# Loading ak, b and rv as whole 128-row tiles instead of two 40-row halves, without the start memsets (delta-rule attention followed by a GELU MLP, one core)

## The chip, the cores and the metric

The kernel runs on one core of a Trainium2 chip, in one launch. The metric is the device time of one execution in microseconds. The three runs of the kernel before took 675.35, 676.0 and 679.76 us, a median of 676.0 us. All tensors are 32-bit floats.

## The reference, cut to what matters

The first block is a recurrent attention over 768 time steps, for 4 batches of 8 heads with a head size of 40. The second is a two-layer MLP over the 3072 tokens that the first gives.

```python
state = np.zeros((B, H, D, D))                  # B, H, S, D = 4, 8, 768, 40
for t in range(S):
    y[:, :, t] = np.einsum('bhd,bhde->bhe', rt, state)
    Sa = np.einsum('bhde,bhe->bhd', state, at)
    state_decay = state * wt[:, :, None, :] - np.einsum('bhd,bhe->bhde', Sa, bt)
    state = state_decay + np.einsum('bhd,bhe->bhde', vt, kt)
x = y.transpose(0, 2, 1, 3).reshape(B * S, H * D)   # 3072 x 320
h = x @ w_in                                        # 320 -> 2048
g = h * (1.0 / (1.0 + np.exp(-1.702 * h)))
return g @ w_out                                    # 2048 -> 320
```

## The kernel before, in words

The sequence is cut into 12 chunks of 64 steps. A chunk is worked on for two batches at a time, so there are 24 units (chunk, batch pair). Inside a unit the recurrence is turned into matrix work: cumulated decays (`decay`), scores between the steps of the chunk (`prep`, tiles ps_A, ps_RV, and ps_N in `inverse`), the inverse of a triangular 64x64 matrix per head by repeated squaring (`inverse`, tile ps_level, with transposes EX on VectorE in between), and the update of the state and the outputs (`solve`, tiles ps_B, ps_X, ps_y). After each second unit a chunk of tokens is complete, and its MLP (`mlp`, tiles ps_up and ps_down) becomes available as matmul work between the units.

TensorE (PE) works on tiles of 64x64 or less, four of them beside each other, so a tile has two halves of 64 partitions. For the tensors that are laid out by channel, each half holds one head's 40 channels in its first 40 rows, and 24 rows that are zero.

Four things matter for the change:

- **The loads (L495 to L505).** For each unit i, `load(i)` plans five transfers, all issued on SP's queue: ak (a and k side by side, 128x1024 elements in SBUF), b (128x512), rv (r and v, 128x1024), RV (v by time, 128x320) and time (128x640). RV and time are loaded as 128 rows in one transfer. Of ak, b and rv only the rows 0 to 39 and 64 to 103 are loaded, in two transfers of 40 rows each (L498 to L503, `HALF` is rows 0 to 63 and 64 to 127). In HBM these three tensors have 128 rows per unit, with zeros in the 48 others. A row is 4096 bytes for ak and rv, and 2048 bytes for b. Each of the three has two buffers in SBUF, used in turn by even and odd units.
- **The memsets (L334, L335, L339, L340, L348, L349).** VectorE (DVE) sets both buffers of ak and both of b to zero at the start, since the element operations of `prep` (L619, L621, L624) run over all 128 rows. The buffers of rv are not set: only their 40-row parts are read, by matmuls.
- **The order.** `ORDER` (L107 on) lists all planned tasks by number, in one order that was written out ahead; each engine executes its own tasks in that order. SP's queue carries all loads, the weights (`weight`, L469: raw 64-bit pieces of 128x320 elements of the MLP's weights, 32 transfers, all of them among the first loads), the stores of the MLP's input to HBM and its loads back (L971, L975), and the stores of the result (L1019). The program gives the transfers eight completion semaphores in turn: before a transfer is issued, SP waits until the transfer eight places ahead of it has landed, besides waiting until its buffer is free.
- **The weights.** The MLP's weights come as 64-bit floats and are turned into 32-bit ones on ACT (L447), DVE (L451, L455, L459) and POOL (L463) in the first part of the run.

Unit 0's path at the start goes: logw is loaded and its logarithm taken (L526), PE cumulates it (ps_cumc), ACT makes the decay factors FT and GT (L565), DVE multiplies ak by GT and FT (L624, L619) and b by GT (L621), and PE computes ps_RV, ps_A and ps_N. Every matmul is issued by the helper `mm`, so PE's rows all bear L300.

Of the kernel before, what the change touches and what calls it, by code (L numbers as in the profile page):

```python
# [248 lines left out]
def rwkv7_gelu_quick(ctx: ExitStack, tc: tile.TileContext, time_d, v_d, w_d, wc_d, ak_d, b_d, rv_d, w_in, w_out, out):  # L249
    nc = tc.nc  # L250
    H, D, S = 8, 40, out.shape[0] // 4
# [17 lines left out]
    HALF = [slice(0, 64), slice(64, 128)]  # L269
# [10 lines left out]
    plan = Plan(dict(logw=3, wc=3, G=1, wch=3, wz=2, time=2, ak=2, b=2, rv=2, FT=3, GT=1, kh=2, bh=2, zr=2, rz=2,  # L280
                     A=1, B=1, RV=2, E0=2, W0=2, P21=2, PT=2, W=2, E=2, ES=2, EX=2, T=2, Tc=1, QT=1, zraw=2, zT=1, M=2, x=1, xT=3, g=4, ob=1), 4)
# [44 lines left out]
    def of(e):  # L326
        return nc.gpsimd if e == "POOL" else nc.vector


    def several(name, shape):  # L330
        return [single(f"{name}{i}", shape) for i in range(plan.slots[name])]

    ak_t, b_t, rv_t = several("ak", [128, 2, 8, 64]), several("b", [128, 8, 64]), several("rv", [128, 2, 8, 64])
    def padded(engine, t):  # L334
        engine.memset(t, 0.0)  # L335

    nc.scalar.preload_act_table_set("natural_log_exp_and_others")

    padded(nc.vector, ak_t[0])  # L339
    padded(nc.vector, b_t[0])  # L340
    full = work.tile([128, 128], FP32, tag="g0", name="full")
    make_identity(nc, full)
    ident = single("ident", [128, 64])
# [1 line left out]
    one32, two32 = single("one32", [128, 32]), single("two32", [128, 32])  # L345
    nc.vector.tensor_add(one32, ident[:, :32], ident[:, 32:])
    nc.vector.tensor_add(two32, one32, one32)
    padded(nc.vector, ak_t[1])  # L348
    padded(nc.vector, b_t[1])  # L349

    def select(t, compare, base, sign, fill):

# [142 lines left out]
    def load(i):  # L495
        for name, of, src, n in (("ak", ak_of, ak_d, 1024), ("b", b_of, b_d, 512), ("rv", rv_of, rv_d, 1024),
                                 ("RV", RV_of, v_d, 320), ("time", time_of, time_d, 2 * DM)):
            rows = [slice(p.start, p.start + D) for p in HALF] if name in ("ak", "b", "rv") else [slice(0, 128)]  # L498

            def go(t, name=name, of=of, src=src, rows=rows):  # L500
                for p in rows:
                    dst = of(i)[p, 8:].rearrange("p g j n -> p (g j n)") if name == "RV" else of(i)[p]
                    nc.sync.dma_start(dst, src[i, p])  # L503
            plan.add(10 * i - 4, {"SP": 350.0 * len(rows)}, go, writes=[(name, i)] + ([("v", i)] if name == "RV" else []),
                     size=sum(p.stop - p.start for p in rows) * n * 4)  # L505


    G_of = lambda i: buf("G", i, [128, 2, 160])
# [527 lines left out]
    for i in range(2):  # L1036
        logarithm(i)
    load(0)
    load(1)
    weights()  # L1040
    for i in range(NU):
        decay(i)
        if i + 3 < NU:
            load_w(i + 3)
        if i + 2 < NU:
            logarithm(i + 2)
        if i >= 2:
            load(i)
        prep(i)
        inverse(i)  # L1050
        solve(i)
        if i % 2:
            mlp(i // 2)
# [84 lines left out]
```

## Time and profile before

| What | Value |
|---|---|
| median of three runs | 676.0 us (675.35 to 679.76) |
| span of the profiled execution, its own time | 676.5 us |
| PE busy | 648.5 us, 96% |
| DVE busy | 444.6 us, 66% |
| ACT busy | 331.6 us, 49% |
| POOL busy | 175.3 us, 26% |
| share of 16 DMA engines in hardware queue q1 | 32.6% |
| read from HBM, written to it | 59.15 MB, 7.86 MB |
| mean granted TensorE clock | 0.994 |

The page's span runs from the first to the last instruction; nothing of the execution is shown outside of it. A row of the windows view gives a stretch of time, its length, then for each engine the busy time and the number of instructions, then the granted clock of TensorE (PEclk), the mean busy share of the 16 DMA engines, and the rate at which they moved data. A row of the timeline gives a start, a length, the engine, the line, the operation, the tile written and those read, and in brackets how long the engine had been idle before and what released it. SPq is SP's queue; its rows are issues of transfers. Where transfers overlap, the busy share can exceed 1.

### The profile page before, as it was taken

The numbers are of one execution on the slowest core, as the hardware profiler recorded it, in microseconds if no ns is written. First come the engines' busy times: TensorE is split into PE (matmuls) and PEld (weight loads), VectorE is DVE, ScalarE is ACT, GpSimd is POOL, SyncE is SP. The second block draws the span as 40 slices with busy tenths as digits, with TensorE's granted clock in tenths as the row PEclk, the third lists the DMA queues.
The fourth block names the chain that finished last, engine by engine and source line by source line (L and its number), as shares of the span: only waits on it lengthen the run. The fifth ranks groups of instructions, "written<-read, shape, count | busy, mean of one in ns | idle before, by whom it ended". The sixth has DMA issues, their size and how long they took to land.

```text
span 676.5 us, 42217 instructions
## 1 busy us (share of the span) xinstructions
PE 648.5 (96%) x19488; PEld 553.4 (82%) x19488; DVE 444.6 (66%) x908; ACT 331.6 (49%) x710; POOL 175.3 (26%) x204
## 2 busy tenths in 40 slices
PE   5768999999999999999999999999999999999997
PEld 5657887987998987788888888798888798798785
DVE  4786787777867667767776587768656766675001
ACT  4676755534564655664545445455454354252110
POOL 6344244224123123123123211322412421300000
PEclk9899999999999999999999999999999999999999
DMA  7983736315314314432404413513412411200200
GB/s 230 300 289 94 232 107 187 103 43 154 108 47 149 93 58 117 121 108 72 118 22 132 141 34 109 156 33 108 140 39 71 122 53 54 61 14 15 61 12 20
DMA packets 35313, 69.74 MB, mean 103 GB/s; under 512 B 5440, under 2 KB 14656, under 8 KB 35136
## 3 DMA queue, kind: packets, MB, share of 16 engines
q1 hardware_dynamic: 35136, 67.03, 32.6%
q8 instruction: 153, 2.51, 1.5%
q14 instruction: 24, 0.20, 0.1%
HBM read 59.15 MB, written 7.86 MB: 99 GB/s over the span
## 4 chain that ended last, share of the span: by engine, by line
PE 93%; DMA 2%; DVE 2%; issue 1%; ACT 1%; DVEq 0%; SPq 0%; ACTq 0%
PE ps_up L300 31%; PE ps_down L300 30%; PE ps_level L300 9%; PE ps_y L300 5%; PE ps_B L300 5%; PE ps_X L300 2%; PE ps_N L300 2%; PE ps_rz L300 2%; PE ps_RV L300 2%; PE ps_A L300 2%; PE ps_zT L300 1%; DMA ak<-in_ak 1%; PE ps_cum L300 1%; PE ps_T L300 1%; DMA b<-in_b 1%
## 5 line engine op out<-in xcount | busy, mean ns | idle before, releaser
L300 PE MATMUL ps_up<-xT_all,w_sb 64*64 64x256 f32 x3840 | 251.0, 377 | 0.8 <-issue 0.4
L300 PE MATMUL ps_down<-w_sb,g 64*64 64x320 f32 x3072 | 237.0, 430 | 0.2 <-ACT zr L877 0.2
L300 PEld LDWEIGHTS ps_up<-xT_all,w_sb 64*64 64x64 f32 x3840 | 170.1, 133 | 15.9 <-issue 1.5
L300 PEld LDWEIGHTS ps_down<-w_sb,g 64*64 64x64 f32 x3072 | 128.0, 133 | 42.8 <-ACT zr L877 0.4
L996 ACT ACTIVATE g<-ps_up 128x1024 f32<-128x1024 f32 x48 | 49.2, 1024 | 45.4 <-PE ps_up L300 45.0
L715 POOL TENSOR_TENSOR EX<-ES,quads 128x512 f32<-128x512 f32 x29 | 38.3, 1322 | 112.7 <-DVE ES L708 74.9
L300 PEld LDWEIGHTS ps_level<-W,EX 64*64 64x64 f32 x2560 | 57.8, 134 | 6.7 <-DVE T L838 0.5
L758 ACT COPY W<-ps_level 128x512 f32<-128x512 f32 (+1 forms) x56 | 29.5, 527 | 67.7 <-PE ps_level L300 65.7
L760 DVE TENSOR_TENSOR E<-two,ps_level 128x256 f32<-128x256 f32 x80 | 33.1, 415 | 34.2 <-ACT W L758 30.1
L300 PE MATMUL ps_level<-W,EX 64*64 64x64 f32 (+1 forms) x2560 | 55.4, 217 | 0.1
L713 ACT ACTIVATE EX<-ES,quads 128x256 f32<-128x256 f32 x80 | 36.3, 501 | 31.0 <-DVE ES L708 30.3
L619 POOL TENSOR_TENSOR ak<-ak,FT 128x512 f32<-128x512 f32 x16 | 20.9, 1305 | 76.6 <-DMA ak<-in_ak 53.4
L708 DVE STREAM_TRANSPOSE ES<-E 128x256 f32<-128x256 f32 x80 | 35.3, 443 | 4.4
L300 PE MATMUL ps_level<-PT,EX 64*64 64x64 f32 (+2 forms) x1280 | 32.8, 235 | 5.1 <-DVE EX L729 3.7
L300 PEld LDWEIGHTS ps_level<-PT,EX 64*64 64x64 f32 x1280 | 30.8, 139 | 8.3 <-DVE EX L729 4.2
L300 PE MATMUL ps_y<-M,bh 64*64 64x104 f32 (+1 forms) x768 | 35.6, 250 | 0.7 <-DVE M L915 0.4
L300 PE MATMUL ps_y<-RV,kh 64*64 64x104 f32 (+1 forms) x768 | 35.6, 251 | 0.0
L899 ACT COPY B<-ps_B 128x416 f32<-128x416 f32 (+1 forms) x34 | 16.6, 492 | 33.4 <-PE ps_B L300 33.2
L300 PEld LDWEIGHTS ps_y<-RV,kh 64*64 64x64 f32 x768 | 28.3, 137 | 2.6 <-DVE M L915 0.5
L689 DVE COPY_PREDICATED PT<-within,ps_N 128x256 f32<-128x256 uint32 x40 | 17.8, 444 | 18.5 <-ACT P L697 13.5
L915 DVE TENSOR_TENSOR M<-ps_X,later 128x832 f32<-128x832 f32 (+1 forms) x24 | 23.8, 993 | 8.3 <-PE ps_X L300 8.1
L300 PE MATMUL ps_B<-RV,A 64*64 64x104 f32 (+1 forms) x768 | 27.9, 252 | 1.1 <-issue 1.1
(131 smaller groups left out, 1088.2 us busy)
## 6 DMA issues: line engine op xcount, KB each, us to landing
ak<-in_ak SPq DMA_DIRECT2D x48, 160.0 KB
rv<-in_rv SPq DMA_DIRECT2D x48, 160.0 KB
time<-in_time SPq DMA_DIRECT2D x24, 320.0 KB
xT_all<-x_dram SPq DMA_DIRECT2D x48, 160.0 KB
wc<-in_wc SPq DMA_DIRECT2D x20, 264.0 KB
logw<-in_w SPq DMA_DIRECT2D x24, 160.0 KB
RV<-in_v SPq DMA_DIRECT2D x24, 160.0 KB
b<-in_b SPq DMA_DIRECT2D x48, 80.0 KB
```

The lines of the kernel that those rows point to most:

```text
L300: nc.tensor.matmul(o, lhsT, rhs, start=start, stop=True, skip_group_check=True)
L619: plan.add(R, {"DVE": 690.0, "POOL": 1270.0, "sbuf": True}, lambda t: of(t.engine).tensor_mul(ahT(), ahT(), FT_of(i)), reads=T("ak", "FT") ...
L689: plan.add(R, dve(256), lambda t, n=n: nc.vector.copy_predicated(tiles_of(at(E0_t, i)), every(within_of(n), [128, 2, 4, 32]), blocks(psum( ...
L708: plan.add(rank, dve(256), lambda t: nc.vector.transpose(ES(n), source(t)), writes=[key("ES", n, 6)], **reads)
L713: nc.scalar.activation(dst[:, :, h], ES(n), ACT.Copy, scale=quads[:, h, :1])
L715: of(t.engine).tensor_mul(dst, ES(n).unsqueeze(2).to_broadcast([128, 8, 2, 32]), quads.unsqueeze(1).to_broadcast([128, 8, 2, 32]))
L758: plan.add(rank, any2(512 - 8 * past), lambda t: copy(t.engine)(tiles_of(W(n + 1))[:, :, :, past:], blocks(psum(t, ""), 64)[:, :, :, past: ...
L760: plan.add(rank, dve(256), lambda t: nc.vector.tensor_sub(tiles_of(E(n + 1)), every(two32, [128, 2, 4, 32]), blocks(psum(t, ""), 64)[:, :, ...
L899: plan.add(R, any2(4 * wide), lambda t: copy(t.engine)(dst(), some(psum(t, "")[:, :, :208])), writes=[("Bv", i)] if x and c > 0 else T("B" ...
L915: plan.add(R + 1, dve(8 * wide), lambda t: nc.vector.tensor_tensor(M_of(i)[:, :, :wide].rearrange("p (j b) n -> p b j n", b=2), some(psum( ...
L996: plan.add(-45, {"ACT": 1030.0, "table": "gelu"}, lambda t: nc.scalar.activation(g_of(c * NQ + q).rearrange("p m r n -> p r m n"), psum(t, ...
```

## The change

All three tensors are loaded like RV and time: one transfer of 128 rows for each tile, which brings the zero rows along. So there are 72 transfers in place of 144, and the four memsets on DVE are gone. The list of tasks and `ORDER` stay as they are; one task that issued two transfers now issues one. The instructions of PE, ACT and POOL and their order are the same; DVE loses the four memsets alone.

```diff
-    def padded(engine, t):
-        engine.memset(t, 0.0)
-
     nc.scalar.preload_act_table_set("natural_log_exp_and_others")
 
-    padded(nc.vector, ak_t[0])
-    padded(nc.vector, b_t[0])
     full = work.tile([128, 128], FP32, tag="g0", name="full")
...
-    padded(nc.vector, ak_t[1])
-    padded(nc.vector, b_t[1])
...
     def load(i):
         for name, of, src, n in (("ak", ak_of, ak_d, 1024), ("b", b_of, b_d, 512), ("rv", rv_of, rv_d, 1024),
                                  ("RV", RV_of, v_d, 320), ("time", time_of, time_d, 2 * DM)):
-            rows = [slice(p.start, p.start + D) for p in HALF] if name in ("ak", "b", "rv") else [slice(0, 128)]
-
-            def go(t, name=name, of=of, src=src, rows=rows):
-                for p in rows:
-                    dst = of(i)[p, 8:].rearrange("p g j n -> p (g j n)") if name == "RV" else of(i)[p]
-                    nc.sync.dma_start(dst, src[i, p])
-            plan.add(10 * i - 4, {"SP": 350.0 * len(rows)}, go, ...)
+            def go(t, name=name, of=of, src=src):
+                dst = of(i)[:, 8:].rearrange("p g j n -> p (g j n)") if name == "RV" else of(i)
+                nc.sync.dma_start(dst, src[i])
+            plan.add(10 * i - 4, {"SP": 350.0}, go, ...)
```

More of the change, by code (lines that the diff above doesn't have):

```diff
@@ L497, in load @@
                                  ("RV", RV_of, v_d, 320), ("time", time_of, time_d, 2 * DM)):
-            rows = [slice(p.start, p.start + D) for p in HALF] if name in ("ak", "b", "rv") else [slice(0, 128)]
-            def go(t, name=name, of=of, src=src, rows=rows):
-                for p in rows:
-                    dst = of(i)[p, 8:].rearrange("p g j n -> p (g j n)") if name == "RV" else of(i)[p]
-                    nc.sync.dma_start(dst, src[i, p])
-            plan.add(10 * i - 4, {"SP": 350.0 * len(rows)}, go, writes=[(name, i)] + ([("v", i)] if name == "RV" else []),
-                     size=sum(p.stop - p.start for p in rows) * n * 4)
+            def go(t, name=name, of=of, src=src):
+                dst = of(i)[:, 8:].rearrange("p g j n -> p (g j n)") if name == "RV" else of(i)
+                nc.sync.dma_start(dst, src[i])
+            plan.add(10 * i - 4, {"SP": 350.0}, go, writes=[(name, i)] + ([("v", i)] if name == "RV" else []), size=128 * n * 4)
     G_of = lambda i: buf("G", i, [128, 2, 160])
```

## The prediction, made before the result was known

> **What bounds the kernel now.** I read the page first, then the stretches, then what PE waits for, then the start of the queues. The first two lines are the span and PE's busy time; then three stretches that make up the whole run, and a few short ones.
>
> ```profile
> span 676.5 us, 42217 instructions
> PE 648.5 (96%) x19488; PEld 553.4 (82%) x19488; DVE 444.6 (66%) x908; ACT 331.6 (49%) x710; POOL 175.3 (26%) x204
> ```
> ```profile
> 0.00:70.00 70.00, 48.31 (x1745) 42.89 (x1749) 47.84 (x80) 43.34 (x117) 33.22 (x61) 0.95 0.72 226
> 70.00:600.00 530.00, 528.52 (x16199) 451.05 (x16200) 376.64 (x778) 273.54 (x570) 142.08 (x143) 1.00 0.33 98
> 600.00:676.50 76.50, 71.70 (x1555) 59.50 (x1546) 20.07 (x53) 14.76 (x25) 0.00 (x0) 0.99 0.09 24
> 2.00:50.00 48.00, 31.77 (x1107) 28.04 (x1108) 33.69 (x58) 29.30 (x81) 24.34 (x43) 0.96 0.89 286
> 10.00:15.00 5.00, 3.71 (x106) 3.74 (x110) 2.79 (x4) 2.03 (x6) 1.75 (x2) 1.00 0.90 263
> 30.00:35.00 5.00, 3.69 (x149) 2.90 (x140) 4.44 (x10) 2.38 (x8) 3.33 (x3) 1.00 1.03 358
> 70.00:75.00 5.00, 5.00 (x128) 4.59 (x125) 2.66 (x5) 3.82 (x8) 0.82 (x1) 1.00 0.92 322
> ```
>
> PE is idle for 676.5 - 648.5 = 28.0 us. Of this, 70.0 - 48.31 = 21.7 us lie in the first 70 us, 1.5 us in the 530 us that follow, and 4.8 us in the tail, which loads nothing of ak, b or rv. From 70 us on PE waits for next to nothing, while the DMA engines stand at 0.33: loads that land somewhat earlier or later there don't show. So the change decides itself in the first 50 us or so, the head. There the DMA engines are at 0.89 of their time on average and move 286 GB/s: the weights and the first units' loads come together.
>
> **The head, step by step.** Issues of transfers by SP, then DVE, then PE, and POOL for the second and third unit's ak:
>
> ```profile
> 0.81 0.41 SPq L492 DMA_DIRECT2D logw<-in_w  x1
> 2.03 0.69 SPq L503 DMA_DIRECT2D ak<-in_ak  x2
> 2.76 0.71 SPq L503 DMA_DIRECT2D rv<-in_rv  x2
> 3.51 0.36 SPq L503 DMA_DIRECT2D RV<-in_v  x1
> 4.39 0.73 SPq L503 DMA_DIRECT2D b<-in_b  x2
> 25.50 0.73 SPq L503 DMA_DIRECT2D ak<-in_ak  x2
> ```
> ```profile
> 1.09 0.91 DVE L335 MEMSET ak<- 128x1024 f32 x1 [1.09 <-PEq L1131]
> 2.06 0.48 DVE L335 MEMSET b<- 128x512 f32 x1
> 7.29 0.72 DVE L619 TENSOR_TENSOR ak<-ak,FT 128x512 f32<-128x512 f32 x1
> 9.27 0.69 DVE L650 TENSOR_TENSOR RV<-ps_RV,upper 128x512 f32<-128x512 f32 x1 [1.25 <-PE ps_RV L300]
> 10.25 0.78 DVE L621 SCALAR_TENSOR_TENSOR b<-b,GT 128x512 f32<-128x512 f32 x1 [0.29 <-DMA b<-in_b]
> ```
> ```profile
> 8.01 1.02 PE L300 MATMUL ps_RV<-rv 40*64 40x64 f32 x27 [0.53 <-DMA rv<-in_rv]
> 11.29 1.14 PE L300 MATMUL ps_N<-b,ak 40*64 40x64 f32 x32 [1.30 <-DVE b L621]
> ```
> ```profile
> 16.03 1.26 POOL L624 TENSOR_TENSOR ak<-ak,GT 128x512 f32<-128x512 f32 x1 [4.28 <-DMA ak<-in_ak]
> 32.57 1.26 POOL L624 TENSOR_TENSOR ak<-ak,GT 128x512 f32<-128x512 f32 x1 [1.67 <-PE ps_level L300]
> ```
>
> The first ak is issued at 2.03, just after its memset ends (1.09 + 0.91 = 2.00), though SP was free at 0.81 + 0.41 = 1.22. Its DVE product ends at 7.29 + 0.72 = 8.01. DVE then sits idle, since rv lands late (PE reads its second half from 8.01 on), and idle again until b lands at about 10.22. PE's ps_N waits for that product of b.
>
> **The memsets removed.** Two memsets of 0.91 and two of 0.48 us (both buffers alike) make 2.8 us of DVE time, in a stretch where DVE has nothing else to do but small constants; DVE time as such is worth nothing. Their worth is the wait on SP: ak can be issued at 1.25 instead of 2.03, 0.8 us earlier. Nothing is late in their place: no other load waits for them.
>
> **Half the issues.** A pair takes 0.69 to 0.73 us on SP, a single one 0.36 (RV's row), so each load of ak, rv and b saves 0.35 us of issue. For unit 0: logw to 1.22, ak to 1.6, rv to 2.0, RV to 2.4, time to 2.75, b to 3.15, in place of 4.39 + 0.73 = 5.12. Over the run 72 issues fewer are 25 us of SP time, which PE's 1.5 us of idle after 70 us shows to be hidden. SP waits at issue for the transfer eight places ahead; those eight now hold more bytes, so this wait can only come earlier.
>
> **More bytes, and over which engines they are spread.** This is the disputed term. The DMA view lists all transfers, and the page counts the small packets:
>
> ```profile
> ak<-in_ak SPq DMA_DIRECT2D x48, 160.0 KB
> rv<-in_rv SPq DMA_DIRECT2D x48, 160.0 KB
> time<-in_time SPq DMA_DIRECT2D x24, 320.0 KB
> xT_all<-x_dram SPq DMA_DIRECT2D x48, 160.0 KB
> wc<-in_wc SPq DMA_DIRECT2D x20, 264.0 KB
> logw<-in_w SPq DMA_DIRECT2D x24, 160.0 KB
> RV<-in_v SPq DMA_DIRECT2D x24, 160.0 KB
> b<-in_b SPq DMA_DIRECT2D x48, 80.0 KB
> extra<-in_w_out SPq DMA_DIRECT2D x12, 320.0 KB
> x_dram<-x SPq DMA_DIRECT2D x48, 80.0 KB
> out<-ob SPq DMA_DIRECT2D x48, 80.0 KB
> w_sb<-in_w_in SPq DMA_DIRECT2D x8, 320.0 KB
> extra<-in_w_in SPq DMA_DIRECT2D x8, 320.0 KB
> xT_all<-in_w_out SPq DMA_DIRECT2D x4, 320.0 KB
> ```
> ```profile
> DMA packets 35313, 69.74 MB, mean 103 GB/s; under 512 B 5440, under 2 KB 14656, under 8 KB 35136
> ```
>
> There are 412 transfers. Those of 40 rows (ak, rv, b and x_dram, 48 each) are 192, those of 64 or 128 rows 220. No row of data is below 512 B, so the 5440 small packets are marks of completion: 220 x 16 + 192 x 10 = 5440 exactly. I read it as one mark for each engine that takes part: a whole transfer runs on 16 engines, a half on 10, with 4 of its rows on each. If both halves use the same ten, an engine gets 4 + 4 = 8 rows; a whole tile gives 128 / 16 = 8 rows to each of 16. The loaded engines then carry the same bytes as before, and the 60% more fall on six engines that had room. The stretches fit: 10 to 15 us, mostly halves, shows 0.90 and 263 GB/s although loads are queued up, while 30 to 35 us, mostly whole transfers, reaches 1.03 and 358 GB/s.
>
> [...]
>
> Bounds in bytes: in 48 us at 286 GB/s the head moves 13.7 MB. Among it are about eight tiles of ak and rv and six of b, to which 48 rows each are added: 8 x 48 x 4096 + 6 x 48 x 2048 = 2.2 MB, so 15.9 MB (the number of tiles is an estimate from four units' loads, the last one in part). At 358 GB/s this takes 44.4 us, 3.6 less than now; at 331 the same 48 us; at 322 (the stretch 70 to 75, all whole transfers) 49.4, 1.4 more; at 286 55.6, 7.6 more. Whole transfers are nearest to the rows of 322 and 358, whose middle, 340, gives 46.8, 1.2 less. So by bytes the head's end moves by -1.2 us.
>
> **What of it reaches PE.** By unit 0's b, 164 + 524 + 524 + 164 + 328 + 262 KB = 1.97 MB have to come; at 340 GB/s 5.8 us from about 2 us on, so b is there at 7.8, at 263 GB/s at 9.5, against 10.22. DVE is free for it at 8.01 + 0.69 = 8.7, once L650 is done (rv comes before b). So ps_N starts at 8.7 + (11.29 - 10.25) = 9.7 instead of 11.29, 1.6 us earlier; with the slow rate at 10.5, 0.75 earlier. From here on the order is fixed and the units follow in a chain, so the shift stays if the loads keep up. Unit 1's ak has to come 1.6 us before 16.0: 1.97 MB and the w_sb, two logw, rv and ak ahead of it make 3.67 MB, at 340 GB/s 2 + 10.8 = 12.8, in time; at 263 GB/s 16.0, and the shift is lost. Unit 2's ak is issued at 25.50 and used at 32.57: seven microseconds of queueing, where the -1.2 us of the bytes and the earlier issue both help. Bytes give -1.2 and the start -1.6; they are two bounds of one shift and not added. I take -1.6, the place where a row of PE names the wait.
>
> Sum against the profiled execution: 676.5 - 1.6 = 674.9. The profiled span is 0.5 above the median of the runs shown, so 674.4 for the time.
>
> **Rivals.**
> - **Common ceiling (slower).** The DMA engines together don't pass the head's 286 GB/s when rows of 4 KB go to all partitions, or the ten engines were not the same. Then the 2.2 MB are paid in full at the head's end: 676.0 + 7.6 = 683.6. For it: engines at 0.89 already. Against it: 358 in 30 to 35 us. It decides below 331 GB/s over the head; half its price, 679.8, comes at about 308.
> - **Hidden.** The start moves, but DVE's chain through the third unit (4.44 us busy of 5 at 30 to 35 us, with the weights' conversion in it) or a late piece of weight takes it back: 676.0.
> - **Full rate.** All 16 engines keep 358 GB/s through the head, and its end comes 3.6 us earlier: 672.4. [...]
>
> That the change does something else can be left out: the queues hold the same order with one issue for two.
>
> **How the numbers follow.** Forecast 0.50, hidden 0.18, common ceiling 0.20, full rate 0.12. The range leaves out about 1 in 10 on each side: the ceiling beyond two thirds of its price, 681, and below 671, under the full rate's 672.4. About 1%, or 6.8 us, is what a measurement of this kernel can tell from no change. Slower by more than that (over 682.8) is only the ceiling at nearly full price, 0.10; faster (under 669.2) only a rate no row shows, 0.04; the rest, 0.86, is within.
>
> **What would show it.** Right: DVE's first row is no memset, ak's issue at about 1.25, b's product at about 8.7, ps_N at about 9.7; small packets 292 x 16 + 48 x 10 = 5152; 10 to 15 us over 320 GB/s; PE idle in the first 70 us near 20. Wrong: 2 to 50 us still at 286 GB/s or less, ps_N of the later units behind its old place, or new idle time of PE after 70 us, where the text counts none.

## The result and the profile after

The changed kernel takes 684.4 us (median of five runs, 681.56 to 686.49), the kernel before 677.62 (five runs, 675.35 to 679.76). The ratio is 1.0107, with a 95% interval of 1.0075 to 1.0139: slower by 1.07%, where the prediction had 674.4 us and a small gain, and 671 to 681 as its range. The profiled execution of after took 686.49 us, of which 684.3 are its span; it is the longest of the five.

From the page of after, the span, the busy times, and the DMA packets with the row of the data queue:

```profile
span 684.3 us, 42040 instructions
PE 651.9 (95%) x19488; PEld 587.7 (86%) x19488; DVE 442.2 (65%) x904; ACT 332.1 (49%) x710; POOL 174.1 (25%) x204
...
DMA packets 38478, 81.51 MB, mean 119 GB/s; under 512 B 5152, under 2 KB 14368, under 8 KB 38304
...
q1 hardware_dynamic: 38304, 78.83, 35.9%
```

The traffic is as foretold: 5152 marks of completion, and 78.8 MB instead of 67.0. PE's idle time is 684.3 - 651.9 = 32.4 us, 4.4 more than before; its busy time, which takes in short gaps between matmuls whose ends are modelled (a matmul's row lasts 0.29 us in the mean, and its starts lie some 33 ns apart), grew by 3.4. Together that is the 7.8 us between the spans. The stretches of after (the head, what follows, and three short ones):

```profile
0.00:70.00 70.00, 45.95 (x1692) 41.04 (x1695) 41.95 (x71) 41.02 (x108) 31.43 (x61) 1.00 0.70 249
70.00:600.00 530.00, 526.68 (x16002) 468.91 (x15997) 375.78 (x771) 271.90 (x571) 141.44 (x143) 1.00 0.38 117
10.00:15.00 5.00, 4.55 (x116) 4.28 (x117) 2.29 (x4) 2.88 (x12) 1.01 (x1) 1.00 1.03 408
20.00:25.00 5.00, 4.98 (x140) 4.79 (x140) 2.55 (x5) 2.12 (x5) 0.87 (x1) 1.00 0.13 42
```

In the 530 us after the head PE gets through 16002 matmuls, before it was 16199: at 530 / 16199 = 33 ns each, the 197 that are missing are 6.4 us. So most of the loss is made where the prediction looked for nothing. And the DMA engines can move more than the head of before asked of them: 408 GB/s from 10 to 15 us, more than any 5 us of before, and nearly nothing to do from 20 to 25. The granted clock isn't the cause: its mean is 0.998 in after and 0.994 in before. Nor does the longer busy time of PEld go with the loss: it is 587.7 us here against 553.4, but 580.0 in a kernel below that is as fast as before (after without rv).

What PE waited for in the whole run. In after:

```profile
PE ps_level L300 <- issue: 4.9, 5, 1.4
PE ps_cum L300 <- ACT logw L515: 3.8, 1, 3.8
PE ps_level L300 <- DVE EX L718: 3.7, 3, 1.7
PE ps_y L300 <- issue: 2.6, 1, 2.6
PE ps_RV L300 <- DMA rv<-in_rv: 2.0, 1, 2.0
PE ps_zT L300 <- issue: 1.5, 1, 1.5
PE ps_cum L300 <- issue: 1.4, 1, 1.4
```

and the four largest waits on "issue" in before:

```profile
PE ps_cum L300 <- issue: 2.1, 1, 2.1
...
PE ps_B L300 <- issue: 1.1, 1, 1.1
...
PE ps_rz L300 <- issue: 0.8, 1, 0.8
...
PE ps_level L300 <- issue: 0.6, 2, 0.3
```

"Issue" is time in which PE waits for nothing that the profile shows. The four rows of after make 10.4 us, the four of before 4.6; with the shorter ones it is 12.4 against 5.9. No engine and no load of data grew like this. Most of this growth lies in the first 70 us, where other waits shrank; from 70 us on "issue" has 2.8 us in after and 1.2 in before, and from 70 to 600 us all other waits together have 0.4 and 0.6.

Something that PE needs and that isn't in a row of its own is its instructions. The page lists them among the DMA queues, as q8 instruction: 153 packets, 2.51 MB and 1.5% of 16 engines, in before and after alike, so 16 KB each. PE's 38976 weight loads and matmuls, by 153, make 255 for each packet, so these packets are PE's. How far they are hidden is what the next rows show. The DMA queues of after in four stretches, the first two at the start (packets, MB, share of 16 engines):

```profile
q1 hardware_dynamic: 1541, 3.42, 101.1%
```
```profile
q1 hardware_dynamic: 400, 0.82, 100.6%
q8 instruction: 1, 0.02, 3.2%
```

From 5 to 13.85 us the engines are full with loads (101.1%) and no instruction packet starts; the first starts at 13.87, with the engines still full (100.6%). PE had by 10.4 us started as many instructions as in before by the start of its first packet, so this one is some 3.5 us late. What let it start then, the rows don't show. PE falls idle on "issue" at 14.99 (first row), and again later (second row), here with the issue of b by SP before it:

```profile
16.42 1.07 PE L300 MATMUL ps_level<-PT,EX 64*64 64x96 f32 x18 [1.43 <-issue]
```
```profile
321.37 0.38 PE L300 MATMUL ps_level<-PT,EX 64*64 64x64 f32 x9 [0.89 <-issue]
```
```profile
316.87 0.33 SPq L493 DMA_DIRECT2D b<-in_b  x1
```

The queues around this second stall, from 315.02 to 318.98 us, and from there to 322:

```profile
q1 hardware_dynamic: 130, 0.25, 24.7%
```
```profile
q1 hardware_dynamic: 157, 0.53, 48.7%
q8 instruction: 1, 0.02, 1.8%
```

b is 128 rows of 2 KB, 0.26 MB, and the first row holds 0.25 MB: as b ends, the instruction packet starts at 318.98; it takes 0.9 us (1.8% of 16 engines' 3.02 us), and PE goes on at 321.37, 1.5 us after its end. At the start the packet of 13.87 took 1.1 us (3.2% of 16 engines' 2.14 us), and PE goes on 1.4 us after its end. In before the corresponding first packet starts at 9.93; from 5 to 9.92 us, and from 9.93 to 12, its queues show:

```profile
q1 hardware_dynamic: 699, 1.33, 93.8%
```
```profile
q1 hardware_dynamic: 290, 0.54, 80.5%
q8 instruction: 1, 0.02, 3.5%
```

The link holds for more than these two stalls. Before, after and the fourteen kernels below run the same instructions of PE. In their traces PE has 167 waits of 0.15 us or more on "issue", and every one ends 1.2 to 1.8 us after the end of an instruction packet; of its 254 other waits 15 do. Counting packets k and PE's weight loads and matmuls from 0, the one that ends such a wait is number 441 + 254 k, to within 24. So these waits are for the instructions that the packet brings. 15 of the 153 packets of after and 8 of those of before have one behind them: most packets come in time, and not all.

It also holds for what is too short for a list of waits. The start of each matmul in after can be set against the start of the same matmul in before. After is 1.6 us behind at 80 us and 7.7 at the end. Of the 6.1 us between, 5.1 are lost at matmuls that start 1.2 to 1.8 us after the end of a packet, which are 14% of them. Each trace is one execution, though: those of the four kernels below that are as fast as before also lose 1.9 to 4.2 us after 80 us against this one of before, so the figure says where time goes, and the runs say how much.

So theory A: the added load traffic holds up PE's instruction packets. The rivals were that the loss is made by the first units' loads in the head (the prediction's common ceiling), that it depends on which DMA engines the loads run on (engine theory below, against the bytes theory, by which the bytes count wherever they go), or on how a load is cut.

### The profile page after: what moved, and what is told of

It is laid out like the page before. It is cut to its first block, busy times and chain, and to the rows that moved or that the text cites. A ratio compares the mean times of both kernels' runs of the same rounds, so it can differ in the third digit from the quotient of the medians.

```text
span 684.3 us, 42040 instructions
## 1 busy us (share of the span) xinstructions
PE 651.9 (95%) x19488; PEld 587.7 (86%) x19488; DVE 442.2 (65%) x904; ACT 332.1 (49%) x710; POOL 174.1 (25%) x204
## 2 busy tenths in 40 slices
DMA packets 38478, 81.51 MB, mean 119 GB/s; under 512 B 5152, under 2 KB 14368, under 8 KB 38304
## 3 DMA queue, kind: packets, MB, share of 16 engines
q1 hardware_dynamic: 38304, 78.83, 35.9%
q8 instruction: 153, 2.51, 1.5%
## 4 chain that ended last, share of the span: by engine, by line
PE 92%; issue 3%; DVE 2%; ACT 1%; DMA 1%; SPq 0%; DVEq 0%; ACTq 0%
PE ps_up L300 31%; PE ps_down L300 30%; PE ps_level L300 9%; PE ps_y L300 5%; PE ps_B L300 5%; PE ps_X L300 2%; PE ps_RV L300 2%; PE ps_N L300 2%; PE ps_A L300 2%; PE ps_rz L300 2%; PE ps_zT L300 1%; PE ps_cum L300 1%; DMA rv<-in_rv 1%; PE ps_T L300 1%; PE ps_Q L300 1%
## 5 line engine op out<-in xcount | busy, mean ns | idle before, releaser
L300 PE MATMUL ps_up<-xT_all,w_sb 64*64 64x256 f32 x3840 | 254.7, 377 | 0.9 <-issue 0.5
L300 PE MATMUL ps_down<-w_sb,g 64*64 64x320 f32 x3072 | 243.4, 430 | 0.2 <-ACT zr L866 0.2
L300 PEld LDWEIGHTS ps_up<-xT_all,w_sb 64*64 64x64 f32 x3840 | 178.1, 133 | 11.3 <-issue 1.8
L300 PEld LDWEIGHTS ps_down<-w_sb,g 64*64 64x64 f32 x3072 | 152.0, 133 | 24.5 <-issue 0.4
L300 PEld LDWEIGHTS ps_level<-W,EX 64*64 64x64 f32 x2560 | 60.5, 134 | 4.9 <-DVE T L827 0.5
L300 PE MATMUL ps_level<-PT,EX 64*64 64x64 f32 (+2 forms) x1280 | 35.2, 241 | 8.9 <-issue 4.1
L300 PEld LDWEIGHTS ps_level<-PT,EX 64*64 64x64 f32 x1280 | 32.8, 142 | 12.3 <-issue 5.0
L300 PEld LDWEIGHTS ps_y<-RV,kh 64*64 64x64 f32 x768 | 30.8, 133 | 4.4 <-issue 2.8
L616 POOL TENSOR_TENSOR kh<-time,G 128x320 f32<-128x320 f32 x18 | 16.1, 892 | 55.0 <-PE ps_y L300 27.6
L300 PEld LDWEIGHTS ps_y<-M,bh 64*64 64x64 f32 x768 | 29.3, 133 | 0.6 <-DVE M L904 0.6
```

The lines of the kernel that those rows point to most:

```text
L300: nc.tensor.matmul(o, lhsT, rhs, start=start, stop=True, skip_group_check=True)
L616: plan.add(R + 4, {"POOL": 870.0, "DVE": 490.0, "sbuf": True}, lambda t, n=n, dst=dst: of(t.engine).tensor_mul(dst(i)[:, :, :D], by_head(t ...
```

## The experiments

Each verdict is a ratio to before, run beside it on the same chip, with its 95% interval. One row of the trace is used for several kernels: the ACT activations that write g, 48 in all, with the start of the first and of the last. Their distance is the length of the MLP stage, which starts behind the head. It is 577.5 us in before and 583.6 in after:

```profile
L996 ACT ACTIVATE g<-ps_up x48: 1023/1023/1042, 80.3 to 657.8; 128x1024 f32<-128x1024 f32 x48
```
```profile
L985 ACT ACTIVATE g<-ps_up x48: 1024/1025/1039, 81.9 to 665.5; 128x1024 f32<-128x1024 f32 x48
```

It comes from one execution each. The four kernels below that are within 0.2% of before give 578.5, 580.3, 581.0 and 581.7, so differences under some 4 us say nothing.

**Where the loss is made.** Whole tiles for the first two units alone:

```diff
-            rows = [...halves...] if name in ("ak", "b", "rv") else [slice(0, 128)]
+            rows = [...halves...] if name in ("ak", "b", "rv") and i >= 2 else [slice(0, 128)]
```

(and no memsets, since the first whole tile brings the zero rows).

> Whole tiles for units 0 and 1 alone (their zero rows fill the buffers, so the memsets are gone), two 40-row halves from unit 2 on. Theory A (the whole loads delay TensorE's instruction fetches, which run over the same DMA engines, wherever they are; most of the loss comes from the units after the first): the steady loss goes, the faster start stays, 675 to 678 us, against 677.6 for before and 684.4 for after. Theory B (the loss is made in the first 50 us by the first whole loads): 682 to 685 us.

Measured: 0.9996 (0.9968 to 1.0023), 680.05 against 680.56 us. The first units' whole loads cost nothing on balance, and gain nothing. The other side of this, halves for units 0 to 3 and whole tiles after that (`and i < 4` in the same place, memsets kept):

> Halves for units 0 to 3, whole tiles from unit 4 on, memsets kept: the head is that of before, all that follows that of after. Traffic theory: 0.7 to 1.1% slower than before, nearly all of after's loss. Common ceiling of the prediction (the loss is made in the first 50 us): within 0.3% of before.

Measured: 1.0071 (1.0044 to 1.0098). Its stage is 582.9 us long, near that of after, though by itself too near the 581.7 above to tell:

```profile
L996 ACT ACTIVATE g<-ps_up x48: 1024/1025/1042, 80.6 to 663.5; 128x1024 f32<-128x1024 f32 x48
```

By the medians two thirds of the loss come from the units from 4 on, and the first two give none that is seen (to 0.3%). The interval overlaps that of the whole change, and units 2 and 3 were not tried alone, so what they add stays open. The theory that the loss is made in the head falls for its main part.

**The memsets.** After, with the four memsets put back in their old places:

> After with the four memsets put back. The prediction's start: ak is issued 0.8 us later, ps_N of unit 0 begins 0.3 to 0.9 us later than in after, 10.7 to 11.3 us; 684 to 686 us in all. If the memsets matter in another way (SBUF, order of the queue), more than 2 us off after.

Measured: 1.0111 (1.0078 to 1.0144), after alone 1.0107. They are worth nothing that can be seen. The expectation of the start missed: ak is issued at 2.03 again, yet ps_N begins before its place in after (10.44), not behind it:

```profile
9.89 1.14 PE L300 MATMUL ps_N<-b,ak 40*64 40x64 f32 x32 [0.58 <-DVE b L617]
```

**Traffic without anything that depends on it.** Before, with additional loads from unit 4 on into a spare tile that nobody reads. By the marks of before (10 for a transfer of 40 rows, 16 for one of 128) once on ten engines, once on 16:

```diff
+                if name == "rv" and i >= 4:
+                    for k in (0, 40, 80):
+                        nc.sync.dma_start(spare[k:k + 40], rv_d[i, k:k + 40]...[:, :896])
```
```diff
+                if name == "rv" and i >= 4:
+                    nc.sync.dma_start(spare, rv_d[i]...[:, :896])
```

> [...] If the added bytes slow the fetches wherever they go (bytes theory): 0.7 to 1.2% slower, like after, in the time from 100 us on.

> Before, and from unit 4 on one more transfer of 128 rows of 3584 bytes for each unit into a spare tile: 459 KB more a unit, on all 16 engines. Engine theory: slower than before by 0.5 to 1%, and clearly slower than with three times 40 rows. Bytes theory: the same as with three times 40 rows.

Measured: 1.0163 (1.0122 to 1.0204) with three times 40 rows, 1.0104 (1.0070 to 1.0138) with 128. Loads that no instruction waits for cost as much as the change did, and more as three transfers on ten engines. The theory that it matters whether the other six are left free falls (if the ten are the same each time, which no row shows), and added loads as such are shown to cost. Their stages are 595.2 and 590.7 us long:

```profile
L1001 ACT ACTIVATE g<-ps_up x48: 1015/1024/1040, 81.2 to 676.4; 128x1024 f32<-128x1024 f32 x48
```
```profile
L1000 ACT ACTIVATE g<-ps_up x48: 1023/1024/1041, 80.5 to 671.2; 128x1024 f32<-128x1024 f32 x48
```

A second way shows here beside the instructions: the loads of the MLP's input, which have to come through the same queue, are late for PE. From PE's waits with three times 40 rows, and with 128:

```profile
PE ps_up L300 <- DMA xT_all<-x_dram: 3.3, 3, 1.5
```
```profile
PE ps_up L300 <- DMA xT_all<-x_dram: 1.4, 2, 1.3
```

After itself has no such wait. From 70 to 600 us PE's waits for engines and data make 5.7 and 3.0 us here, against 0.6 in before and 0.4 in after. So the loss of these two is only in part of the change's kind: of the 18.1 and 13.3 us that their traces lose against before's after 80 us, 8.6 and 8.1 lie 1.2 to 1.8 us behind instruction packets. They also add issues to SP's queue, three and one a unit, which was not separated from the bytes.

**Whole tiles at the old traffic.** After without the loads of rv from unit 4 on (`if i >= 4 and name == "rv": return` ahead of the transfer; stale r and v are used, the same instructions run), and before without them:

> After, but rv isn't loaded from unit 4 on (stale r and v are used): 786 KB a unit of ak, b and rv instead of 1311, a little under the 819 of before, all as whole tiles. Traffic theory: within 0.4% of before, its loss gone. If whole tiles as such (128 partitions, all 16 engines, zero rows) slow something: still 0.5 to 1% slower than before.

> Before, but rv isn't loaded from unit 4 on (stale r and v are used, the same instructions run): 328 KB a unit fewer on the DMA engines. Traffic theory (each load delays TensorE's instruction fetches, whichever engines it uses): faster than before by 0.3 to 0.7%, since before has such stalls too. If before is free of them after the first 70 us, as its waits view says: within 0.2% of before.

Measured: 1.0016 (0.9993 to 1.0040) for after without rv, whose stage is 580.3 us long, and 1.0010 (0.9988 to 1.0032) for before without it.

```profile
L987 ACT ACTIVATE g<-ps_up x48: 1024/1024/1039, 78.2 to 658.5; 128x1024 f32<-128x1024 f32 x48
```

Whole tiles, 128 partitions, 16 engines and zero rows cost nothing that can be seen (to 0.4%) while the bytes of ak, b and rv a unit stay at those of before. But taking traffic away from before gains nothing either: the 0.3 to 0.7% that theory A promised there were not found. The loss is not proportional to traffic. It looks as if before stood near the end of a flat part; no run looks for that end.

**How the bytes are cut.** After's bytes in two halves of 64 rows (no memsets), and halves of 48, 52 and 60 rows (memsets kept), where `D` in the row slices of L498 becomes that number. The 13 and 15 engines for 52 and 60 rows are the author's estimate, from 4 rows on each engine as the marks of before give for 40 rows:

> The bytes of after (all 128 rows), but as two transfers of 64 rows, no memsets. Each runs on 16 engines with 4 rows on each, where a whole tile puts 8 rows on each at once. Theory A1 (the added bytes, or the six engines that they reach, delay the fetches): 682 to 686 us as after. Theory A2 (a fetch waits behind one transfer's rows on its engine, so the longer run of 8 rows in one transfer is what hurts): 676 to 679 us as before.

> Two halves of 48 rows instead of 40, memsets kept: 16 engines with 3 rows on each per half, instead of 10 engines with 4 rows; a fifth more bytes than before where after has three fifths more. If the fetches run on an engine that the 40-row halves leave alone (theory A1, engine): clearly slower than before, 680 to 685 us, since that engine goes from 0 to 6 rows per tile, after has 8. If the total of bytes counts (theory A1, bytes): a third of the loss, 679 to 680 us. If the fetch's engine is one of the ten: 6 rows instead of 8 on it, 675 to 678 us.

> Halves of 52 rows, memsets kept: 13 engines with 4 rows each. Engine theory: as before if the fetches are on one of the three engines left out; slower by 1 to 2.6% if they are on one of the thirteen and not of the ten. Bytes theory: between before and two halves of 64 rows, 0.6 to 1.5% slower.

> Halves of 60 rows, memsets kept: 15 engines with 4 rows each, 94% of after's bytes. Engine theory, with the fetches on the one engine that is now left out: as before, within 0.4%, while two halves of 64 rows lost 2.6%. Engine theory with the fetches on one of the fifteen, or bytes theory: 1 to 2.6% slower.

Measured: 1.0264 (1.0232 to 1.0296) with 64 rows, 1.0060 (1.0033 to 1.0086) with 48, 1.0076 (1.0048 to 1.0104) with 52, and 1.0136 (1.0099 to 1.0172) with 60. With the halves the loss grows with the rows loaded, whether 16 engines take part (48 and 64 rows, 6304 marks each, worked out further below) or, by the estimate, 13 or 15. No engine stands out, so the theory of one special engine falls a second time, under the same condition and with that estimate. And two halves of 64 rows cost 2.5 times what one tile of 128 rows does. Theory A2, that the longer run of 8 rows in one transfer is what hurts, falls with that. For these halves the data queue's row is, against 35.9% in after for the same bytes:

```profile
q1 hardware_dynamic: 39456, 78.83, 41.1%
```

Why the same bytes take a higher share in this cut was not shown. A part of this loss lies ahead of the MLP stage, which starts at 90.3 us instead of 81.9 in after:

```profile
L989 ACT ACTIVATE g<-ps_up x48: 1016/1026/1042, 90.3 to 682.8; 128x1024 f32<-128x1024 f32 x48
```

The same bytes cut the other way, along the row:

```diff
-                nc.sync.dma_start(dst, src[i])
+                for h in (0, 1):                    # ak, b and rv only
+                    nc.sync.dma_start(part(dst), part(src[i]))   # 128 rows, half the length
```

> After's bytes in two transfers of 128 rows and half the row length each (2048 bytes for ak and rv, 1024 for b), no memsets. Both run on 16 engines with 8 rows each. If two halves of 64 rows lost 2.6% because each goes to 64 partitions: as after here, 1.0 to 1.4%. If it was the number of transfers on 16 engines (144 instead of 72): about 2.6%.

> After's bytes in four transfers of 128 rows and a quarter of the row each (1024 bytes for ak and rv, 512 for b), no memsets. After lost 1.07%, two half rows 0.48%. If a fetch waits behind one transfer's share on an engine (32 KB in after, 16 KB, now 8 KB for ak and rv): 0 to 0.35% slower than before. If the two half rows were better for another reason (two issues fill SP's queue of eight sooner, or the start): 0.4% or more, or worse again with twice the issues.

Measured: 1.0048 (1.0031 to 1.0065) with two half rows, 1.0161 (1.0130 to 1.0192) with four quarter rows. As a forecast of the time, the idea that an instruction packet waits behind one transfer's share on an engine missed with the second, and wasn't borne out. Both rows of g show why the two are not to be read as one series:

```profile
L990 ACT ACTIVATE g<-ps_up x48: 1011/1024/1043, 78.2 to 662.0; 128x1024 f32<-128x1024 f32 x48
```
```profile
L990 ACT ACTIVATE g<-ps_up x48: 1007/1023/1041, 86.8 to 671.6; 128x1024 f32<-128x1024 f32 x48
```

The stage is 583.8 and 584.8 us long, as in after; the difference lies ahead of it, at 78.2 against 86.8, and 81.9 in after. With four issues a tile PE waits longer at the start: 2.5 us for b's product of the first units, where after has 0.9. So the time of the quarter rows doesn't settle the idea: from 70 us on, "issue" has 2.8 us in after, 1.7 with half rows and 1.3 with quarter rows, in one execution each. PE's waits with the quarter rows have, among others:

```profile
PE ps_N L300 <- DVE b L615: 2.5, 1, 2.5
...
PE ps_N L300 <- POOL ak L613: 2.2, 2, 1.6
```

In the heads of the quarter rows and of the 64-row halves the granted clock also stood lower, at 0.86 and 0.82 from 2 to 50 us, against 1.00 in after; what of their loss in the head is due to that was not separated.

**A version with the better start.** Units 0 and 1 whole in two half rows each, no memsets, 40-row halves from unit 2 on:

> Units 0 and 1 whole, each tile as two transfers of 128 rows and half a row, no memsets; 40-row halves from unit 2 on. It puts the better start of the half rows (its trace was 1.2 to 1.8 us ahead of before until 150 us) before the traffic of before, which cost nothing. If the share theory holds: 0.1 to 0.4% faster than before. If the start is regained later: within 0.1%.

Measured: 0.9990 (0.9962 to 1.0019). The earlier start is not a gain that can be told from none. No version was found that beats before.

## Why the prediction was wrong, point by point

- **What bounds the kernel: the failed step.** "From 70 us on PE waits for next to nothing, while the DMA engines stand at 0.33: loads that land somewhat earlier or later there don't show. So the change decides itself in the first 50 us or so, the head." The first half was right of before, and taking traffic away confirmed it. The second half doesn't follow: it asked only whether PE waits for the loads, and left out what else uses the DMA engines and the queue. So the sum had no term for the added bytes after the head. Loads from unit 4 on that nobody reads cost 1.0 and 1.6%, and the change alone from unit 4 on 0.71%; in after's trace 6.1 of the 7.7 us are lost after 80 us, 5.1 of them just behind instruction packets.
- **Memsets and start.** From after, the issue of the first ak, DVE's products of RV and of b, and PE:

```profile
1.29 0.42 SPq L493 DMA_DIRECT2D ak<-in_ak  x1
```
```profile
8.78 0.69 DVE L639 TENSOR_TENSOR RV<-ps_RV,upper 128x512 f32<-128x512 f32 x1 [0.60 <-PE ps_RV L300]
9.40 0.89 DVE L610 SCALAR_TENSOR_TENSOR b<-b,GT 128x512 f32<-128x512 f32 x1
```
```profile
7.51 1.13 PE L300 MATMUL ps_RV<-rv 40*64 40x64 f32 x32 [2.01 <-DMA rv<-in_rv]
10.44 1.13 PE L300 MATMUL ps_N<-b,ak 40*64 40x64 f32 x32 [0.94 <-DVE b L610]
```

  The issue at 1.25 was right (1.29). ps_N came 0.85 us earlier, not 1.6: the sum let L650 (here L639) start at 8.0, but rv landed only at 7.5 and DVE had to wait for ps_RV until 8.78. The direction was right and its size half. That the memsets are behind it isn't borne out: with them back, ps_N began at 9.89, which leaves the halved issues and the loads. What follows the start took it back: the first instruction packet at 13.87 instead of 9.93 alone cost a stall of 1.43 us.
- **Issues on SP.** Worth nothing after the head, as said. With four issues a tile instead of one PE waited 2.5 us for b's product in the first 70 us, 0.9 in after, though what the issues alone cost was not separated.
- **Bytes and engines.** The count of marks was right: 5152 in after, and with halves of 48 rows 220 x 16 + 48 x 10 + 144 x 16 = 6304, as its page has. The halves of 64 rows have the same: of the 39456 packets of their row 38304 - 5152 = 33152 are data, as in after, which leaves 6304. The rate came in part: 408 GB/s from 10 to 15 us, where over 320 was asked for, but over the head, where the sum took 340, it was 303. From after:

```profile
2.00:50.00 48.00, 31.72 (x1055) 28.10 (x1058) 28.54 (x49) 27.86 (x79) 21.46 (x42) 1.00 0.84 303
```

  That a mark stands for an engine is a reading, and that both halves use the same ten no row shows. What was concluded, that six engines with room make the added bytes harmless, was wrong.
- **The rival that ended on this side.** The common ceiling gave 683.6 us, close to the 684.4 measured, and it was not what happened. Its condition was a rate below 331 GB/s over the head, and 303 is below it. But this is no ceiling: it is the mean of stretches with 408 and with 42. And the rival has the whole price paid by the head's end, while after is 1.6 us behind at 80 us, and the first two units' whole loads cost nothing. The number agrees by accident, and the experiment with whole tiles from unit 4 on tells this best.
- **Places to look.** PE's idle time in the first 70 us rose to 24.1 instead of falling to 20, and after 70 us it rose from 1.5 to 3.3: the first had been named as a sign of being right and the second as one of being wrong, and both speak against the forecast.

What is shown: added load traffic slows this kernel, also where nobody reads it, mostly after the head, and the shape of whole tiles doesn't. The traces show besides that PE's waits on "issue" are waits for its instruction packets (167 of 167), and that after 80 us after loses its time just behind them. The listed waits on "issue" from 70 us on go with the loss in the main: 7.9 us with halves of 64 rows, 5.8 and 3.6 with the loads that nobody reads, 5.5 with halves of 60, 2.8 in after, 2.4 with whole tiles from unit 4 on, at most 1.2 in before and in three of the four kernels that are as fast. Against it stand the halves of 48 and 52 rows, with 0.4 at most for a loss of 0.6 and 0.8% (in traces of their fastest executions), and the fourth kernel as fast as before, with 2.1.

What is not isolated is that the loads are what makes the packets late. Of the two stalls that are worked out above, one packet started as a load ended, the other with the engines still full, and no experiment took the packets out of the way. What stays open: why an instruction packet has to wait for loads at all, and why taking traffic away from before gains nothing.

## What to carry to other kernels

DMA engines that were 33% busy weren't free here: ask what else travels on them, above all the instructions of TensorE, which took 255 of them every 4.4 us (38976 instructions and 676.5 us by 153 packets), and test it with a load that nobody reads. Loading zeros to save issues and memsets was here a trade of something that was hidden for something that wasn't. And a total that agrees with a rival is no proof of the rival; put the change into one part of the run at a time.

## What the runs showed of the hardware that was not expected

- One instruction packet of 16 KB moved in about 1 us (0.9 to 1.7 in after), and when PE waited for one, it went on only 1.2 to 1.8 us after its end, in all 167 waits of 16 traces. With loads filling the DMA engines (101.1%) none started from 5 to 13.85 us in after; the next started with them still full (100.6%).
- The same bytes to the same tiles cost 0.48, 1.07, 1.61 or 2.64% over before, as two half rows, one tile, four quarter rows or two halves of 64 rows, a part of it in the head.
- The DMA engines moved 408 GB/s over 5 us in after (10 to 15 us), mostly in rows of 4 KB and of 2.5 KB; no stretch shown of before went over 358.
